# A Fourier transform and two expert layers in one kernel: GpSimd makes the block sums of x2, asb goes ahead of the difference on VectorE, and the two weighings of a pair stand two rounds apart

## The chip, the core and the metric

The kernel runs on one core of a Trainium2 chip. A core has five engines that run side by side, each through its own instructions in a fixed order: TensorE (PE in the profile, its weight loads PEld), VectorE (DVE), ScalarE (ACT), GpSimd (POOL) and SyncE (SP, which here starts transfers). They wait for each other by semaphores. The metric is the device time of one execution in microseconds (us). Three runs of the kernel before took 2791.44, 2799.14 and 2800.77 us, a median of 2799.14 us.

## The reference

Three things are computed one after the other, in float32:

```python
X = np.fft.fft(x, axis=1); X = np.fft.fft(X, axis=2)   # x is 8 x 3072 x 256
x1 = X.real.reshape(8 * 3072, 256)
h = x1 @ w_in                     # 256 -> 2048
x2 = (h - np.tanh(h)) @ w_out     # 2048 -> 256
h = x2 @ w_in2                    # 256 -> 1024
e = np.exp(h - h.max(-1)); sm = e / (e.sum(-1) + 1e-9)
solu = h * sm
ln = (solu - mean(solu)) / np.sqrt(var(solu) + 1e-6) * g_ln
out = ln @ w_out2                 # 1024 -> 256
```

## The kernel before, in words

**Precision.** A float32 value is split into a rounded half and a rest. ScalarE makes the rounded half (`rnd`, L166), and VectorE or GpSimd makes the rest by a subtraction (`rest`, L169). A product then takes three matmuls: high by high, high by low, low by high.

**Stages.** The first part of the program does the transform along the sequence. The main loop, which takes nearly the whole time, runs over 48 groups (`n`, `NG`) of 256 pairs of tokens and, in each, over the 16 blocks of 128 columns of the first hidden layer (`j`, `NM`). One pass of the loop body is called a step here, 16 steps of one `n` a big round; steps are numbered 0 to 15 in it. (The short title of the change says "round" for a step.)

**One step on the first layer.** TensorE first adds the odd part of the hidden block of the step before (`parity(.., 1)`, L879, 3 matmuls) and then starts the even part of this step's block (`even`, L879, 3 matmuls) in one of three PSUM buffers `h`. VectorE makes the first half of `h` of the step before (`act_in`, L904, written over the odd half), the sum `asb` of this step's even part and a correction (`lead`, L897), and, for the block of two steps before, the difference of `h` and its tanh (`act_out`, L921). The odd part of a block may be added only after `asb` has read its even part, so TensorE waits for `asb` at the start of the next step. ScalarE takes the tanh (L912) and rounds the difference into the high half of `gh` (L166); the low half of `gh` comes from GpSimd (L169), or, for the two blocks in eight that `LOWS` names, from VectorE (`low_by_vector`). Three steps after a block was started, its `gh` goes through six matmuls into `x2p` (`o1`, L941); the last two of the six need the low half.

**The second layer.** When the 16 blocks of a group are done, `x2p` holds x2 for 512 tokens, four tiles `t` of 128 tokens, handled as two pairs `p` of tiles 2p and 2p+1. The product of a pair with `w_in2` is done by Strassen's scheme with seven block products instead of eight: the four blocks A11, A12, A21, A22 of x2 (`xb`) and the four sums S1 to S4 (`sum_x2`, L957, one instruction for both pairs of a group) are split into high and low halves (`split_x2`: ScalarE the high, GpSimd the low, tile `xs`), three splits for each pair. TensorE multiplies them into two PSUM banks (`product`, L970), with `xs` as the loaded weights and the low half in the third pass. VectorE copies and combines the banks to `u` (`block`, L992). Then, for each tile: the exponential (`power`, ScalarE, L1007), the product of `u` and the exponential with its sum (`weigh`, VectorE, L1016, 128x1024, both inputs in SBUF), the square with its sum (`square`, ScalarE, L1027), three small steps for the scale (`scale`, GpSimd, L1035 to L1041), the transpose of 32x32 blocks (`turn`, VectorE, L1046, with a transfer out and back in four parts on SyncE's queue), the splits of the turned tile (`split_moved`, ScalarE and GpSimd, tile `ut`), the output product (`outp`, TensorE, L1074 and L1081), and the scaled store (`scaled`, `store`, L1091, L1095).

**What sets the order.** It is written out by hand. `layer2` is called at three places of each step ("ahead", "early", "late") with lists of (`back`, work): the work of pair `p` is issued in step 20 + `back` + 8p of the loop. So `back` 8, 9, 10 and 12 mean steps 4, 5, 6 and 0 of a big round for even p, and 12, 13, 14 and 8 for odd p. Each engine takes its instructions in the order in which the steps issue them; nothing reorders them later.

Of the kernel before, what the change touches and what calls it, by code (L numbers as in the profile page):

```python
# [32 lines left out]
NG = B * GPB  # L33
# [106 lines left out]
def fft2_moe_moe_kernel(  # L140
    ctx: ExitStack, tc: tile.TileContext, xr, x8, xn, xn8, w_in, w_out, w_in2, w_out2, g_ln, tt, t8, ft, out
):
    nc = tc.nc
# [725 lines left out]
    bank_b = p_pr.tile([P, HF], F32, tag="b", name="bank_b")  # L869

    hs, as_, ts_, gs = {}, {}, {}, {}
    LOWS = (0, 5)
    x2p, x2s = {}, {}

    def parity(n, m, u):
# [19 lines left out]
    def lead(n, m):  # L895
        asb = as_[n, m] = wk1.tile([P, GP], F32, tag="asb", name=f"asb{n}_{m}")
        nc.vector.scalar_tensor_tensor(  # L897
            out=asb, in0=zg[n][1], scalar=wnu[:, m : m + 1], in1=hs[n, m][:, 0], op0=ALU.mult, op1=ALU.add
        )
# [52 lines left out]
    def sum_x2(b):  # L952
        a0, a1, op = {
            S1: (A21, A22, ALU.add), S2: (S1, A11, ALU.subtract),
            S3: (A11, A21, ALU.subtract), S4: (A12, S2, ALU.subtract),
        }[b]
        nc.vector.tensor_tensor(out=xb[:, b], in0=xb[:, a0], in1=xb[:, a1], op=op)  # L957

    def split_x2(p, b0, b1):
        x = xb[:, b0 : b1 + 1, p % 2]  # L960
# [52 lines left out]
    def weigh(t, h=None):  # L1013
        e, st = es.pop(t), sts[t]
        u = us[t][0]
        nc.vector.scalar_tensor_tensor(  # L1016
            out=u, in0=u if h is None else h, scalar=-1.0 if h is None else 1.0, in1=e,
            op0=ALU.mult, op1=ALU.mult, accum_out=st[:, 2:3],
        )
        us[t] = (u, e)  # L1020

    def square(t):

        u, e = us[t]
        st = sts[t]
        nc.scalar.activation(out=st[:, 3:4], in_=st[:, 2:3], func=AF.Copy, scale=-1.0 / (32 * FF2))
        nc.scalar.activation(  # L1027
            out=e, in_=u, func=AF.Square, scale=1.0 / 32, bias=st[:, 3:4], accum_out=st[:, 6:7]
        )

    def scale(t):

        st = sts[t]
        g = nc.gpsimd
        g.tensor_scalar(  # L1035
            out=st[:, 4:5], in0=st[:, 1:2], scalar1=1e-9, scalar2=1e-3, op0=ALU.add, op1=ALU.mult
        )
        g.tensor_scalar(
            out=st[:, 5:6], in0=st[:, 4:5], scalar1=st[:, 4:5], scalar2=st[:, 6:7], op0=ALU.mult, op1=ALU.add
        )  # L1040
        g.tensor_tensor(out=st[:, 10:11], in0=st[:, 5:6], in1=mhalf, op=ALU.pow)  # L1041
# [66 lines left out]
    def layer2(step, place):  # L1108

        works = {  # L1110
            "ahead": (
                (20, lambda p: store(2 * p + 1)),
                (24, lambda p: store(2 * p)),
                (2, lambda p: product(p, bank_a, A12, B21)),
                (4, lambda p: product(p, bank_b, S3, T3)),
                (6, lambda p: product(p, bank_b, A22, T4)),
                (1, lambda p: nc.scalar.copy(out=bank_b, in_=bank_a)),
                (3, lambda p: (new_u(2 * p), kept(2 * p, 1))),
            ),
            "early": (  # L1120
                (17, lambda p: outp(2 * p + 1, 0)),
                (19, lambda p: outp(2 * p + 1, 1)),
                (21, lambda p: outp(2 * p, 0)),
                (23, lambda p: outp(2 * p, 1)),
                (3, lambda p: block(2 * p, 0, bank_a, False, True)),
                (5, lambda p: block(2 * p + 1, 1, bank_a, True, True)),
                (6, lambda p: block(2 * p + 1, 0, bank_b, False, False)),
                (7, lambda p: block(2 * p, 1, bank_a, True, False)),
                (7, lambda p: power(2 * p + 1)),
                (8, lambda p: (power(2 * p), weigh(2 * p + 1))),  # L1130
                (9, lambda p: weigh(2 * p)),
                (10, lambda p: (square(2 * p + 1), scale(2 * p + 1), turn(2 * p + 1))),
                (12, lambda p: (square(2 * p), scale(2 * p), turn(2 * p))),
                (14, lambda p: split_moved(2 * p + 1, 0)),
                (16, lambda p: split_moved(2 * p + 1, 1)),
                (18, lambda p: split_moved(2 * p, 0)),
                (20, lambda p: split_moved(2 * p, 1)),
                (-1, lambda p: split_x2(p, A11, A12)),
                (1, lambda p: split_x2(p, S2, S3)),
                (3, lambda p: split_x2(p, A22, S4)),  # L1140
            ),
            "late": (
                (0, lambda p: product(p, bank_a, A11, B11, True)),
                (2, lambda p: product(p, bank_b, S2, T2)),
                (4, lambda p: product(p, bank_a, S1, T1, True)),
                (6, lambda p: product(p, bank_a, S4, B22)),
                (4, lambda p: (new_u(2 * p + 1), kept(2 * p + 1, 1))),
                (19, lambda p: scaled(2 * p + 1)),
                (23, lambda p: scaled(2 * p)),
            ),  # L1150
        }
        for back, work in works[place]:
            p = pair_at(step, back)
            if p is not None:
                work(p)
# [11 lines left out]
    for step in range(steps + 3):  # L1167
        n, j = divmod(step, NM)
        if step in at_ab:
            special(at_ab[step])  # L1170
        if 0 < step <= steps:
            parity(*divmod(step - 1, NM), 1)
        if step < steps:
            even(n, j)
        if 0 < step <= steps:
            act_in(*divmod(step - 1, NM))
        if n == 0:
            lead(n, j)
        lag = 3 if step < NM else 2
        for s in range(out_done, min(step - lag + 1, steps)):  # L1180
            act_out(*divmod(s, NM))
        out_done = max(out_done, min(step - lag + 1, steps))
        if step - 1 in wo2_at:
            split_wo2(wo2_at.index(step - 1), True)
        layer2(step, "ahead")
        if 0 < n < NG:
            lead(n, j)
        if 0 < n < NG:
            for blk in {3: (S1,), 4: (S2, S3), 5: (S4,)}.get(j, ()):
                sum_x2(blk)  # L1190
        layer2(step, "early")
        if NM <= step < steps + 2:
            low_by_vector(*divmod(step - 2, NM))
        if step in at_o1:
            special(at_o1[step])
        if step in (NM, NM + 2):
            mean_wo2((step - NM) // 2)
        if step == NM + 2:
            nc.tensor.matmul(bank_b, wi2[:, B11, 0, :P], wi2[:, B11, 0], start=True, stop=True)
        s1 = step - 5 if step < NM else step - 3  # L1200
        for s in (range(o1_done, min(s1 + 1, steps))):
            o1(*divmod(s, NM))
        o1_done = max(o1_done, min(s1 + 1, steps))
        layer2(step, "late")
        if step in (3, 5, 7, 9):
            c, part = divmod((step - 3) // 2, 2)
            split_wo1(c + 2, wo1_raw[c + 2], slice(part * 2, part * 2 + 2))
        if step == NM:
            raw1.close()
            mv = pool(mv_stack, "mv", 2, side="right")  # L1210
        if step in wi2_sums:
            sum_wi2(nc.vector, wi2_sums[step])
        if step in wi2_splits:
            split_wi2(nc.gpsimd, wi2_splits[step])
        if step in (2, 3):
            load_wo2(step - 2)
        if step == 3:
            for k in range(2):
                load_wi2(k)
        if 8 <= step < NM:  # L1220
            gain_wo2(step - 8)
        if step in (NM + 3, NM + 4):
            center_wo2(step - NM - 3)
        if step in wo2_at:
            split_wo2(wo2_at.index(step), False)
        if step == NM + 12:
            nc.scalar.copy(out=pas, in_=pa)
        if step == NM + 20:
            special_out()
        if n == NG - 1 and j == 9:  # L1230

            b12 = zp.tile([P, HF], F32, tag="zf", name="b12")
            nc.sync.dma_start(out=b12, in_=wi2_d[0][:, HF:])
        if n == NG - 1 and j == 12:
            split_halves(nc.gpsimd, wt[0][:, 0, 0], wt[0][:, 1, 0], b12)
        if step == NM + 30:
            make_identity(nc, ident)
        if 1 <= n and n + 1 < NG:
            if j == 3:
                load_z(n + 1)  # L1240
            for u in range(2):
                if j == 7:
                    sum_z(n + 1, u, nc.gpsimd)
                if j == 11:
                    whole, hi, lo = by_half(n + 1, u)
                    rnd(hi, whole)
                    rest(nc.gpsimd, lo, whole, hi)
# [158 lines left out]
```

## Time and profile before

| what | value |
|---|---|
| median of three runs | 2799.14 us |
| time of the profiled execution | 2796.38 us |
| its span (first to last instruction) | 2794.6 us |
| granted TensorE clock, share of full speed | 0.996 |
| busy: PE / DVE / ACT / POOL | 96% / 84% / 73% / 70% |
| slices 5 to 39 of 40, busy tenths: PE / DVE / ACT / POOL | 9 / 8 / 7 / 7 |

The span is cut into 40 equal slices in the profile, and from the fifth on they hardly differ: the main loop repeats one pattern. "Busy" of TensorE counts each matmul from its start to its modelled end, and neighbours overlap, so the idle time that matters is found by comparing the starts of matmuls and not by the 96%. One big round is therefore read instruction by instruction below, between 1234 and 1271 us.

### The profile page before, as it was taken

How to read it: one execution, taken by the hardware profiler on the slowest of the kernel's cores; microseconds unless marked ns; L12 is line 12 of the kernel's file. 1: busy time of each engine (PE TensorE's matmuls, PEld its weight loads, DVE VectorE, ACT ScalarE, POOL GpSimd, SP SyncE). 2: the span in 40 equal slices, each digit the busy share in tenths (PEclk: the TensorE clock that was granted, in tenths of full speed). 3: DMA queues.
4: the chain of work that ended last, by engine and by line, in shares of the span. 5: the costliest groups of instructions: out<-in, count | busy, mean ns of one | idle time of the engine just before them, and what ended most of it. 6: DMA issues, size and time to landing. Idle time of an engine off the chain costs nothing.

```text
span 2794.6 us, 47353 instructions
## 1 busy us (share of the span) xinstructions
PE 2675.7 (96%) x15073; PEld 2343.8 (84%) x15073; DVE 2346.1 (84%) x4577; ACT 2030.1 (73%) x3990; POOL 1949.3 (70%) x2121
## 2 busy tenths in 40 slices
PE   9999999999999999999999999999999999999998
PEld 5677888888888888888888888888888888888887
DVE  8978888888888888888888888888888888888885
ACT  3467777777777777777777777777777777777775
POOL 0057777777777777777777777777777777777774
PEclk9999999999999999999999999999999999999999
DMA  9942443434434444443434434344344444434342
GB/s 363 365 156 50 95 99 89 106 88 102 94 89 104 92 99 92 98 99 89 105 87 99 99 89 105 86 105 99 84 103 92 99 92 98 99 84 108 88 99 50
DMA packets 882651, 302.97 MB, mean 108 GB/s; under 512 B 788544, under 2 KB 844144, under 8 KB 879104
## 3 DMA queue, kind: packets, MB, share of 16 engines
q1 hardware_dynamic: 879792, 293.45, 43.4%
q10 hardware_dynamic: 2304, 6.42, 0.6%
q8 instruction: 119, 1.95, 0.3%
q14 instruction: 132, 1.08, 0.1%
q0 software_dynamic: 304, 0.07, 0.0%
HBM read 161.26 MB, written 138.60 MB: 107 GB/s over the span
## 4 chain that ended last, share of the span: by engine, by line
PE 59%; DVE 13%; POOL 12%; ACT 11%; issue 4%; DMA 1%; POOLq 0%; ACTq 0%; SPq 0%; DVEq 0%
PE x2p L941 22%; PE h L879 11%; POOL gh L169 10%; PE po L1074 7%; PE bank_b L970 7%; PE bank_a L970 5%; DVE u L1016 4%; PE po L1081 3%; ACT t L912 3%; ACT e L1007 3%; DVE xb L957 3%; ACT gh L166 2%; POOL ut L169 2%; DVE h L904 2%; PE pz L486 1%
## 5 line engine op out<-in xcount | busy, mean ns | idle before, releaser
L169 POOL TENSOR_TENSOR gh<-t,gh 128x512 fp32r<-128x512 f32 x584 | 891.2, 1526 | 406.7 <-ACT gh L166 343.3
L941 PE MATMUL x2p<-gh,wo 128*128 128x512 f32 x4608 | 1150.4, 383 | 19.1 <-POOL gh L169 15.9
L941 PEld LDWEIGHTS x2p<-gh,wo 128*128 128x128 f32 x4608 | 829.4, 190 | 160.3 <-POOL gh L169 56.7
L912 ACT ACTIVATE t<-h 128x512 f32<-128x512 f32 x762 | 455.1, 597 | 634.0 <-DVE h L904 449.6
L879 PEld LDWEIGHTS h<-zs,wt 128*128 128x128 f32 x4572 | 626.5, 192 | 143.9 <-DVE asb L897 105.5
L879 PE MATMUL h<-zs,wt 128*128 128x256 f32 x4572 | 645.0, 277 | 81.1 <-DVE asb L897 80.3
L904 DVE SCALAR_TENSOR_TENSOR h<-asb,h 128x256 f32<-128x256 f32 x762 | 325.2, 427 | 399.6 <-PE h L879 396.7
L169 POOL TENSOR_TENSOR ut<-um,ut 128x512 fp32r<-128x512 f32 x372 | 479.2, 1288 | 175.5 <-PE x2p L941 133.5
L1074 PE MATMUL po<-wo,ut 128*128 128x512 f32 x1528 | 522.2, 383 | 1.9 <-DVE o L1095 1.1
L1081 PE MATMUL po<-wo,ut 128*128 128x256 f32 x1528 | 416.5, 273 | 0.0
L921 DVE TENSOR_TENSOR t<-h,t 128x512 f32<-128x512 f32 x578 | 394.0, 682 | 0.0
L166 ACT ACTIVATE gh<-t 128x512 fp32r<-128x512 f32 x584 | 367.3, 629 | 5.5 <-DVE t L921 4.3
L897 DVE SCALAR_TENSOR_TENSOR asb<-nb,wnu,h 128x256 f32<-128x256 f32 x762 | 358.7, 471 | 0.7 <-PE h L879 0.6
L1016 DVE SCALAR_TENSOR_TENSOR u<-u,e 128x1024 f32<-128x1024 f32 x188 | 340.7, 1812 | 0.0
L1074 PEld LDWEIGHTS po<-wo,ut 128*128 128x128 f32 x1528 | 289.9, 190 | 32.9 <-DVE o L1095 1.6
L970 PE MATMUL bank_a<-wi,xs 128*128 128x512 f32 x1128 | 310.6, 384 | 0.0
L1081 PEld LDWEIGHTS po<-wo,ut 128*128 128x128 f32 x1528 | 293.4, 192 | 0.2
L169 POOL TENSOR_TENSOR xs<-xb,xs 128x256 fp32r<-128x256 f32 (+1 forms) x282 | 233.7, 829 | 17.9 <-ACT xs L166 9.6
L970 PE MATMUL bank_b<-wi,xs 128*128 128x512 f32 x846 | 229.9, 380 | 0.2 <-POOL xs L169 0.2
L166 ACT ACTIVATE ut<-um 128x512 fp32r<-128x512 f32 x372 | 229.8, 618 | 0.0
L1046 DVE STREAM_TRANSPOSE tb<-u 128x1024 f32<-128x1024 f32 x186 | 229.8, 1235 | 0.0
L970 PEld LDWEIGHTS bank_a<-wi,xs 128*128 128x128 f32 x1128 | 206.7, 190 | 26.1 <-POOL xs L169 0.2
(156 smaller groups left out, 3099.4 us busy)
## 6 DMA issues: line engine op xcount, KB each, us to landing
mv_d<-tb SPq DMA_DIRECT2D x186, 512.0 KB, 3.1
um<-mv_d SPq DMA_DIRECT2D x744, 128.0 KB, 3.8
out<-o SPq DMA_DIRECT2D x192, 128.0 KB, 1.7
x<-xr SPq DMA_DIRECT2D x23, 1024.0 KB, 10.8
zf<-z_d SPq DMA_DIRECT2D x64, 128.0 KB, 3.7
z_d<-zt ACTq DMA_DIRECT2D x16, 392.0 KB, 6.0
wi<-w_in SPq DMA_DIRECT2D x6, 1024.0 KB, 7.4
z_d<-zt SPq DMA_DIRECT2D x16, 384.0 KB, 9.8
```

Of the source, the lines that this page charges most:

```text
L166: nc.scalar.activation(out=o, in_=i, func=AF.Copy)
L169: eng.tensor_tensor(out=o, in0=i, in1=hi.bitcast(F32), op=ALU.subtract)
L879: nc.tensor.matmul(in_pairs(hs[n, m][:, 0]), wt[c][:, hw, u, o : o + P], in_turn(zs[:, hz, u]), start=(u == 0 and i == 0), stop=(i == 2), ...
L897: nc.vector.scalar_tensor_tensor(out=asb, in0=zg[n][1], scalar=wnu[:, m : m + 1], in1=hs[n, m][:, 0], op0=ALU.mult, op1=ALU.add)
L904: nc.vector.scalar_tensor_tensor(out=h[:, 1], in0=as_.pop((n, m)), scalar=2.0, in1=h[:, 0], op0=ALU.mult, op1=ALU.subtract)
L912: nc.scalar.activation(out=t, in_=h, func=AF.Tanh)
L921: nc.vector.tensor_tensor(out=g, in0=h, in1=t, op=ALU.subtract)
L941: nc.tensor.matmul(in_pairs(x2p[n][mt]), wo1[c][:, hw, k, mt * P : (mt + 1) * P], in_turn(gh[:, hg]), start=(m == 0 and i == 0), stop=(m = ...
L970: nc.tensor.matmul(in_pairs(bank), xs[:, hx, xs_at[a]], in_turn(wi2[:, b, hw]), start=(start and q == 0), stop=(q == 2), skip_group_check= ...
L1016: nc.vector.scalar_tensor_tensor(out=u, in0=u if h is None else h, scalar=-1.0 if h is None else 1.0, in1=e, op0=ALU.mult, op1=ALU.mult, a ...
L1074: nc.tensor.matmul(in_pairs(po), ut[:, 0, ks], wo2[:, k].rearrange("p h x n -> p (x n) h"), start=(k == 0), stop=False,)
L1081: nc.tensor.matmul(in_pairs(po[:, :D]), ut[:, 1, ks], wo2[:, k, :, 0].rearrange("p h n -> p n h"), start=False, stop=(k == NK2 - 1),)
```

## The change

Four things are edited in the main loop. `lead`, which makes `asb`, is issued directly behind `act_in` in all big rounds, where it stood behind the differences and the "ahead" list in all but the first. The four sums of x2's blocks go from VectorE to GpSimd, and S2 is issued in step 3 with S1 (S3 in step 4, S4 in step 5, as before). The list of layer 2 puts `turn` of tile 2p+1 at 9 (it was 10) and `weigh` of tile 2p at 10 (it was 9). `LOWS` names blocks 1 and 5 in eight instead of 0 and 5.

```diff
-    LOWS = (0, 5)
+    LOWS = (1, 5)
...
-        nc.vector.tensor_tensor(out=xb[:, b], in0=xb[:, a0], in1=xb[:, a1], op=op)
+        nc.gpsimd.tensor_tensor(out=xb[:, b], in0=xb[:, a0], in1=xb[:, a1], op=op)
...
-                (9, lambda p: weigh(2 * p)),
-                (10, lambda p: (square(2 * p + 1), scale(2 * p + 1), turn(2 * p + 1))),
+                (9, lambda p: turn(2 * p + 1)),
+                (10, lambda p: (weigh(2 * p), square(2 * p + 1), scale(2 * p + 1))),
...
-        if n == 0:
+        if step < steps:
             lead(n, j)
...
         if 0 < n < NG:
-            lead(n, j)
-        if 0 < n < NG:
-            for blk in {3: (S1,), 4: (S2, S3), 5: (S4,)}.get(j, ()):
+            for blk in {3: (S1, S2), 4: (S3,), 5: (S4,)}.get(j, ()):
                 sum_x2(blk)
```

On VectorE, before, from the start of step 4 of big round 23 to its step 6 (`h23_3` is block 3 of group 23, `u87` and `u86` are the tiles 2p+1 and 2p, `tb87` the turned tile, `xb` x2 issues are the sums S2 and S3, then S4):

```order
L904 SCALAR_TENSOR_TENSOR h23_3_15422<-asb23_3_15433,h23_3_15422 128x256
L921 TENSOR_TENSOR t23_2_15427<-h23_2_15388,t23_2_15427 128x512
L1095 SCALAR_TENSOR_TENSOR o82_15457<-po82_15369,st82_14639,o82_15457 128x256
L897 SCALAR_TENSOR_TENSOR asb23_4_15481<-nb23_14824,wnu_123,h23_4_15468 128x256
L957 TENSOR_TENSOR xb_1233<-xb_1233 128x256 x2
L1016 SCALAR_TENSOR_TENSOR u87_15350,st87_15351<-u87_15350,e87_15445 128x1024
L904 SCALAR_TENSOR_TENSOR h23_4_15468<-asb23_4_15481,h23_4_15468 128x256
L921 TENSOR_TENSOR t23_3_15473<-h23_3_15422,t23_3_15473 128x512
L897 SCALAR_TENSOR_TENSOR asb23_5_15515<-nb23_14824,wnu_123,h23_5_15503 128x256
L957 TENSOR_TENSOR xb_1233<-xb_1233 128x256
L1016 SCALAR_TENSOR_TENSOR u86_15278,st86_15279<-u86_15278,e86_15485 128x1024
L904 SCALAR_TENSOR_TENSOR h23_5_15503<-asb23_5_15515,h23_5_15503 128x256
```

And the same stretch of VectorE now:

```order
L904 SCALAR_TENSOR_TENSOR h23_3_15422<-asb23_3_15429,h23_3_15422 128x256
L897 SCALAR_TENSOR_TENSOR asb23_4_15476<-nb23_14825,wnu_123,h23_4_15469 128x256
L921 TENSOR_TENSOR t23_2_15427<-h23_2_15388,t23_2_15427 128x512
L1095 SCALAR_TENSOR_TENSOR o82_15458<-po82_15369,st82_14641,o82_15458 128x256
L1016 SCALAR_TENSOR_TENSOR u87_15350,st87_15351<-u87_15350,e87_15445 128x1024
L904 SCALAR_TENSOR_TENSOR h23_4_15469<-asb23_4_15476,h23_4_15469 128x256
L897 SCALAR_TENSOR_TENSOR asb23_5_15510<-nb23_14825,wnu_123,h23_5_15503 128x256
L921 TENSOR_TENSOR t23_3_15474<-h23_3_15422,t23_3_15474 128x512
L1046 STREAM_TRANSPOSE tb87_15527<-u87_15350 128x1024
L904 SCALAR_TENSOR_TENSOR h23_5_15503<-asb23_5_15510,h23_5_15503 128x256
L897 SCALAR_TENSOR_TENSOR asb23_6_15553<-nb23_14825,wnu_123,h23_6_15546 128x256
L1016 SCALAR_TENSOR_TENSOR u86_15280,st86_15281<-u86_15280,e86_15485 128x1024
```

The three sums are gone, `asb` stands next after `h`, and between the two weighings (L1016) there are now two steps with the transpose in between.

On GpSimd, before, in steps 2 to 6 of the same big round (`gh23_k` is the low half of block k, `ut85_0` and `ut85_1` the halves of a turned tile, `xs` the low halves of x2's blocks, first A11 and A12, then S2 and S3):

```order
L169 TENSOR_TENSOR ut85_0_15404<-um85_15247,ut85_0_15404 128x512
L169 TENSOR_TENSOR gh23_1_15430<-t23_1_15393,gh23_1_15430 128x512
L169 TENSOR_TENSOR xs_1234<-xb_1233,xs_1234 128x256
L169 TENSOR_TENSOR gh23_2_15476<-t23_2_15427,gh23_2_15476 128x512
L169 TENSOR_TENSOR ut85_1_15488<-um85_15247,ut85_1_15488 128x512
L169 TENSOR_TENSOR gh23_3_15511<-t23_3_15473,gh23_3_15511 128x512
L169 TENSOR_TENSOR xs_1234<-xb_1233,xs_1234 128x256
L169 TENSOR_TENSOR gh23_4_15547<-t23_4_15508,gh23_4_15547 128x512
```

And now:

```order
L169 TENSOR_TENSOR gh23_0_15398<-t23_0_15361,gh23_0_15398 128x512
L169 TENSOR_TENSOR ut85_0_15405<-um85_15213,ut85_0_15405 128x512
L957 TENSOR_TENSOR xb_1233<-xb_1233 128x256 x2
L169 TENSOR_TENSOR xs_1234<-xb_1233,xs_1234 128x256
L169 TENSOR_TENSOR gh23_2_15479<-t23_2_15427,gh23_2_15479 128x512
L957 TENSOR_TENSOR xb_1233<-xb_1233 128x256
L169 TENSOR_TENSOR ut85_1_15488<-um85_15213,ut85_1_15488 128x512
L169 TENSOR_TENSOR gh23_3_15513<-t23_3_15474,gh23_3_15513 128x512
L957 TENSOR_TENSOR xb_1233<-xb_1233 128x256
L169 TENSOR_TENSOR xs_1234<-xb_1233,xs_1234 128x256
L169 TENSOR_TENSOR gh23_4_15556<-t23_4_15508,gh23_4_15556 128x512
```

The low half of block 1 has left GpSimd and that of block 0 has come; S1 and S2 (x2), S3 and S4 stand in front of `xs`, of `ut85_1` and of the second `xs`. The order on TensorE and SyncE is the same as before, row for row, and on ScalarE too but for which blocks' `gh` reads `h` instead of `t`.

## Rows read from the trace of the kernel before

**Rows 1.** The page, busy time and share of each engine.

```profile
PE 2675.7 (96%) x15073; PEld 2343.8 (84%) x15073; DVE 2346.1 (84%) x4577; ACT 2030.1 (73%) x3990; POOL 1949.3 (70%) x2121
```

**Rows 2.** Windows, instructions of L897 alone (asb, one per step): stretch, length, busy.

```profile
300.00:2700.00 2400.00, 334.09 (x710) 1.00 0.43 96
```

**Rows 3.** Timeline of PE, steps 4 to 6: start, us, what, [idle before <-releaser].

```profile
1234.69 1.46 PE L941 MATMUL x2p<-gh,wo 128*128 128x512 f32 x6
1235.98 0.81 PE L970 MATMUL bank_a<-wi,xs 128*128 128x512 f32 x3
1236.63 0.83 PE L879 MATMUL h<-zs,wt 128*128 128x256 f32 x6
1237.30 0.38 PE L1074 MATMUL po<-wo,ut 128*128 128x512 f32 x1
...
1238.61 1.46 PE L941 MATMUL x2p<-gh,wo 128*128 128x512 f32 x6
1241.73 0.94 PE L879 MATMUL h<-zs,wt 128*128 128x256 f32 x6 [1.66 <-DVE asb L897]
...
1243.24 1.80 PE L941 MATMUL x2p<-gh,wo 128*128 128x512 f32 x6
1244.87 0.81 PE L970 MATMUL bank_b<-wi,xs 128*128 128x512 f32 x3
```

**Rows 4.** Timeline of DVE, the same steps 4 and 5.

```profile
1234.55 0.43 DVE L904 SCALAR_TENSOR_TENSOR h<-asb,h 128x256 f32<-128x256 f32 x1 [0.86 <-PE h L879]
1234.89 0.68 DVE L921 TENSOR_TENSOR t<-h,t 128x512 f32<-128x512 f32 x1
...
1235.88 0.47 DVE L897 SCALAR_TENSOR_TENSOR asb<-nb,wnu,h 128x256 f32<-128x256 f32 x1
1236.27 1.85 DVE L957 TENSOR_TENSOR xb<-xb 128x256 f32<-128x256 f32 x2
1238.04 2.30 DVE L1016 SCALAR_TENSOR_TENSOR u<-u,e 128x1024 f32<-128x1024 f32 x1
...
1241.59 0.41 DVE L957 TENSOR_TENSOR xb<-xb 128x256 f32<-128x256 f32 x1
1241.93 1.22 DVE L1016 SCALAR_TENSOR_TENSOR u<-u,e 128x1024 f32<-128x1024 f32 x1
```

**Rows 5.** Timeline of POOL, the same steps.

```profile
1236.37 1.47 POOL L169 TENSOR_TENSOR gh<-t,gh 128x512 fp32r<-128x512 f32 x1 [1.09 <-PE x2p L941]
1237.97 1.28 POOL L169 TENSOR_TENSOR ut<-um,ut 128x512 fp32r<-128x512 f32 x1
1242.02 2.26 POOL L169 TENSOR_TENSOR gh<-t,gh 128x512 fp32r<-128x512 f32 x1 [2.77 <-ACT gh L166]
1244.24 0.73 POOL L169 TENSOR_TENSOR xs<-xb,xs 128x256 fp32r<-128x256 f32 x1
```

**Rows 6.** Timeline of all engines, steps 13 and 14, the second half of the round.

```profile
1266.83 1.28 POOL L169 TENSOR_TENSOR ut<-um,ut 128x512 fp32r<-128x512 f32 x1
1266.98 2.22 DVE L1016 SCALAR_TENSOR_TENSOR u<-u,e 128x1024 f32<-128x1024 f32 x1
1268.07 2.25 POOL L169 TENSOR_TENSOR gh<-t,gh 128x512 fp32r<-128x512 f32 x1
1270.38 0.70 PE L941 MATMUL x2p<-gh,wo 128*128 128x512 f32 x2 [0.28 <-POOL gh L169]
```

**Rows 7.** Groups by shape: POOL's operations, count, busy us, mean ns, idle before.

```profile
L169 POOL TENSOR_TENSOR gh<-t,gh 128x512 fp32r<-128x512 f32 x584 | 891.2, 1526 | 406.7 <-ACT gh L166 343.3 <-PE x2p L941 49.9 <-issue 4.0
L169 POOL TENSOR_TENSOR xs<-xb,xs 128x256 fp32r<-128x256 f32 x188 | 138.5, 737 | 14.2 <-ACT xs L166 6.1 <-PE h L879 5.6
L169 POOL TENSOR_TENSOR xs<-xb,xs 128x384 fp32r<-128x384 f32 x94 | 95.2, 1013 | 3.7 <-ACT xs L166 3.6
L272 POOL TENSOR_TENSOR zc<-zf 128x128 f32<-128x128 f32 x184 | 70.1, 418 | 0.0
```

**Rows 8.** Timeline of ACT, step 4: the high half of gh.

```profile
1235.61 0.63 ACT L166 ACTIVATE gh<-t 128x512 fp32r<-128x512 f32 x1
```

## The prediction

> **What bounds the kernel now.** I read the page first, then TensorE's own timeline, then what stood on the other engines where TensorE stopped.
>
> On the page TensorE is busy 96% of the span, far ahead of VectorE with 84%, ScalarE with 73% and GpSimd with 70% [rows 1]. That figure hides its stops, since matmuls overlap. So I compare starts. Six matmuls of `x2p` take 1.29 us (1234.69 to 1235.98), three of a bank 0.65, six of `h` 0.67, and half an output product with the `po` matmuls 1.31 (1237.30 to 1238.61) [rows 3]. Eight steps hold eight times `x2p` and `h`, seven bank products and four output halves: 8 x 1.96 + 7 x 0.65 + 4 x 1.31 = 25.47 us. A big round of 16 steps would take 50.94 us if TensorE never stopped. Its real length comes from counting `asb`, one per step: 710 in 2400 us [rows 2], so 54.08 us. TensorE loses 3.14 us in each big round.
>
> Where? Call T the start of step 4, 0.67 us before the first of [rows 3], 1234.02. The six `x2p` that start at 1238.61 should be followed at 1239.90; the next `h` starts at 1241.73, waiting for `asb`: 1.83 us lost. The six `x2p` at 1243.24 take 1.63 instead of 1.29: 0.34 lost to the low half of `gh` [rows 3]. In the second half of the round the last two `x2p` matmuls start at 1270.38 behind GpSimd's `gh` [rows 6], some 0.45 us late. These three make 2.6 of the 3.14 us; the rest is spread over pauses of a tenth.
>
> The cause of the first stands on VectorE. At T + 0.53 come `h`, the difference, a store's sum and `asb`, 1.72 us for the four (1234.55 to 1236.27), then two block sums that take 1.85 us together, though one alone takes 0.41, and a weighing of 2.30 us that takes 1.22 elsewhere [rows 4]. Sum two stands still while GpSimd has its `gh` (1.47 us), the weighing while GpSimd has `ut` (to 1239.25), and the `gh` dispatched at 1242.02 behind a running weighing takes 2.26 instead of 1.28 [rows 5]. So a VectorE instruction with two SBUF inputs and a GpSimd instruction don't run side by side: one waits until the other is done. [Rows 6] also show who goes first: the weighing dispatched at 1266.98 waits for `ut`, and when that ends it runs before the `gh` that GpSimd dispatched at 1268.07. The Trainium skill says the same of the pair of ports that the two share ("SBUF — State Buffer", Who interferes with whom): an exclusive lock, the loser stands still for the whole instruction. By a shared bandwidth both would have stretched; the trace shows one whole instruction added to the other (2.25 is 1.28 and most of a weighing), and on this I build below.
>
> **The change part by part.** *VectorE loses the sums.* Three of the four stand in steps 4 and 5, 1.85 and 0.41 us before the two weighings [rows 4], and only they and the weighing make `asb` of step 5 late. *`asb` moves up* by two instructions, from T + 1.86 to T + 0.87, where the even part is just done; in step 5 it comes behind `h` alone. *The second weighing* leaves step 5 for step 6, and a transpose takes its place; it has one input, so I take it not to hold GpSimd.
>
> The new order on VectorE, with the same durations: `h` at T + 0.53, `asb`, difference (from 1.26 to 1.94), store, first weighing from T + 2.25 to 3.4. Then `h` at 3.4, `asb` of step 5 done at about 4.2. TensorE wants it at the start of step 6, which is T + 2.61 + 3.27 = T + 5.88. So the 1.83 us are gone with more than 1 us to spare. In the second half of the round the `gh` of step 13 no longer meets a weighing: 1.28 instead of 2.25 [rows 6], which is more than the 0.45 us it was late. The second weighing now meets the `gh` of step 14. By the sums below that one ends about 4.6 us after the start of its step, and TensorE wants it at 3.27 + 0.67 + 1.31 + 0.86 = 6.1. I count nothing lost in the second half.
>
> *GpSimd gets the sums*, and here I expect the new wait. No row shows this sum on GpSimd. The nearest is its subtraction of the same 128x256 size, 737 ns; the bounds are 418 ns for half the size and 1013 ns for one and a half [rows 7]. I take 0.74. S1 and S2 in step 3 are free: the low half of block 1 has left that step for VectorE, where it stands in a step without weighing, and GpSimd idled before step 4 for 1.09 us [rows 5]. S3 and S4 are not free. GpSimd's queue from step 4 on, after T:
>
> - the high half of `gh` (0.63 us, [rows 8]) is done at 1.94 + 0.67 = 2.6; the first weighing has the ports since 2.25. A `gh` behind a weighing ends 1.07 + 1.28 us after the weighing's start ([rows 4, 5]: 1241.93, 1244.28): 4.60.
> - S3 0.74, `ut` 1.28, the next `gh` 1.28, each starting some 0.04 before the last one's recorded end: 7.8. TensorE needs this `gh` for the fifth `x2p` matmul of step 6, at 5.88 + 0.67 + 0.65 + 0.86 = 8.06, less 0.17 for the hand-over (`gh` ended 1244.28, its matmul ran about 1244.45). Just in time.
> - S4 is next, and behind it `xs`, the low halves of S2 and S3. But the second weighing is dispatched at about T + 7.74 (5.88 + 0.53, then `h`, `asb`, difference), while that `gh` runs, and as in [rows 6] goes first: to 8.84. S4 to 9.57, `xs` (0.73) to 10.26, its matmul at 10.43.
>
> TensorE wants these low halves in the third pass of the product S2 x T2, at 5.88 + 0.67 + 0.65 + 1.29 + 0.43 = 8.92. Before, `xs` stood directly behind `gh` (1244.24 to 1244.98) and that product began at 1244.87 [rows 3, 5]: no wait. Now it waits 10.43 - 8.92 = 1.5 us. Behind it GpSimd has `gh`, the scale's steps, `ut`, `xs` and `zc`, and it has caught up by step 10, since TensorE slid by the same 1.5.
>
> The sum: of 3.14 us lost per big round 1.5 remain, so 1.64 are saved. With 45 such rounds (the first two and the last are partly without this work) that is 74 us. From the profiled execution's own 2796.4 us (1.8 outside its span; 0.1% under the median of the three runs, 2799.1) comes 2722 us. With sums of 0.42 us the wait is 0.86 and the time 2694; with 1.01 it is 2.06 and 2748.
>
> The Trainium skill speaks against moving such a sum ("GPSIMD Engine Reference", 4.1 Engine selection): two-input elementwise work belongs on VectorE, GpSimd being about twice as slow. The rows agree in kind, 0.74 to 0.41. By its ratio in 3.1 of that page, 1.96, I estimate a sum at 0.80 us and the time at 2728.
>
> **Rivals.** *No new wait (0.25).* GpSimd has 1.09 and 2.77 us of idle time before its two `gh` [rows 5], and what I put down to one instruction of order could fall out otherwise: if S4 and `xs` get the ports before the second weighing, `xs` ends at 9.2 and TensorE waits 0.45, which gives 2675; without any wait it is 45 x 3.14 = 141 us, 2655. Against it: in [rows 6] the waiting weighing goes first.
>
> *Slow sums eat the gain (0.09).* If a sum on GpSimd takes as long as its mean `gh`, 1.53 us [rows 7], S3 and S4 bring 1.58 more, TensorE waits 3.08 and the time is 2793. Between the bounds' 2748 and this lies most of what I give it, say 2775. It decides from 1.55 us a sum. Against it: 512 elements take 1.28 undisturbed, so 256 can't well take more.
>
> *The wait moves to `gh` and grows (0.06).* With `asb` first, the difference ends 0.39 us later in every step, and so do both halves of `gh`. In the four steps behind weighings GpSimd delivers at the limit (0.34 and 0.45 late now, [rows 3, 6]); if the later weighing of step 6 and 14 doesn't free it there, each of the four loses 0.39, 1.56 in all, on top of 1.5 for `xs` and the old 0.45. That is 3.5 us in place of 3.14, and 2796 + 45 x 0.37 = 2813 us. It decides once the four add up to over 1.2. Against it: a transpose and not a weighing stands there now.
>
> **How the numbers follow.** The forecast as worked out has 0.60, its own range 2694 to 2748. The range of 0.8 takes in the case without a wait and a part of the slow sums: 2655 to 2770. About 0.3% (8 us) can be told from no change. Faster: 0.60 + 0.25 + 0.06 of the second rival, 0.91. Within 0.3%: 0.03. Slower: 0.06.
>
> **What would show it.** Right: `h` on TensorE never waits for `asb`; a big round of 52.4 us; one new wait per round, of a `bank_b` matmul in step 6 for GpSimd's `xs`, about 1.5 us; weighings of 1.2 us in step 4; sums on GpSimd of 0.74, S4 near 1.8 because it is held; the `gh` of step 13 at 1.28. Wrong: rounds of 51 us without that wait (first rival), sums over 1 us (second), or `x2p` waiting for `gh` in several steps (third). If `asb` still holds TensorE, my reading of VectorE's queue is wrong.

## The result, and the profile after

The changed kernel took 2727.7 us in the median of four runs (2725.32 to 2731.39), against 2795.38 us of the kernel before: a ratio of 0.976, 95% interval 0.973 to 0.978. The forecast was 2722 us. The profiled execution has a span of 2729.3 us.

The page, busy time by engine, against [rows 1]: VectorE has lost 146 us, GpSimd has gained 135.

```profile
PE 2650.9 (97%) x15073; PEld 2345.3 (86%) x15073; DVE 2200.1 (81%) x4389; ACT 2035.8 (75%) x3990; POOL 2084.7 (76%) x2309
```

How long is a big round now? Below is the window view of L897 alone (stretch, length, busy, count), from 300 to 2500 us, so that the main loop fills it in every kernel.

```profile
300.00:2500.00 2200.00, 319.66 (x670) 1.00 0.43 99
```

There are 670 steps in 2200 us, so a round of 16 takes 52.54 us. The kernel before has 651 in the same stretch, 54.07 us. The difference of 1.53 us, 45 times, is 69 us.

TensorE's timeline in steps 4 to 6 of one big round, which answers to [rows 3]; step 4 starts at T = 1210.18.

```profile
1210.18 0.83 PE L879 MATMUL h<-zs,wt 128*128 128x256 f32 x6
...
1214.77 1.46 PE L941 MATMUL x2p<-gh,wo 128*128 128x512 f32 x6
1216.07 0.83 PE L879 MATMUL h<-zs,wt 128*128 128x256 f32 x6
1216.73 0.81 PE L970 MATMUL bank_a<-wi,xs 128*128 128x512 f32 x3
1217.38 1.46 PE L941 MATMUL x2p<-gh,wo 128*128 128x512 f32 x6
1218.68 0.59 PE L970 MATMUL bank_b<-wi,xs 128*128 128x512 f32 x2
1220.38 0.48 PE L970 MATMUL bank_b<-wi,xs 128*128 128x512 f32 x1 [1.11 <-POOL xs L169]
```

The `h` of step 6 follows `x2p` after 1.30 us, as the matmuls alone take; before, it came 1.83 us later than that. The six `x2p` at 1217.38 run through in 1.30. The only stop is in front of the third pass of `bank_b`: two passes take 0.43 us, so it was due at 1219.11 and started at 1220.38, 1.27 us late.

VectorE in the same steps, against [rows 4]:

```profile
1211.05 0.48 DVE L897 SCALAR_TENSOR_TENSOR asb<-nb,wnu,h 128x256 f32<-128x256 f32 x1
...
1212.44 1.22 DVE L1016 SCALAR_TENSOR_TENSOR u<-u,e 128x1024 f32<-128x1024 f32 x1
...
1213.91 0.47 DVE L897 SCALAR_TENSOR_TENSOR asb<-nb,wnu,h 128x256 f32<-128x256 f32 x1
...
1214.90 1.24 DVE L1046 STREAM_TRANSPOSE tb<-u 128x1024 f32<-128x1024 f32 x1
...
1217.93 1.81 DVE L1016 SCALAR_TENSOR_TENSOR u<-u,e 128x1024 f32<-128x1024 f32 x1
```

And GpSimd, against [rows 5]:

```profile
1208.82 1.55 POOL L957 TENSOR_TENSOR xb<-xb 128x256 f32<-128x256 f32 x2
1211.00 0.73 POOL L169 TENSOR_TENSOR xs<-xb,xs 128x256 fp32r<-128x256 f32 x1 [0.63 <-PE h L879]
1212.93 1.87 POOL L169 TENSOR_TENSOR gh<-t,gh 128x512 fp32r<-128x512 f32 x1 [1.20 <-ACT gh L166]
1214.76 0.73 POOL L957 TENSOR_TENSOR xb<-xb 128x256 f32<-128x256 f32 x1
1215.45 1.28 POOL L169 TENSOR_TENSOR ut<-um,ut 128x512 fp32r<-128x512 f32 x1
1216.69 1.28 POOL L169 TENSOR_TENSOR gh<-t,gh 128x512 fp32r<-128x512 f32 x1
1217.93 0.73 POOL L957 TENSOR_TENSOR xb<-xb 128x256 f32<-128x256 f32 x1
1218.62 1.70 POOL L169 TENSOR_TENSOR xs<-xb,xs 128x256 fp32r<-128x256 f32 x1
```

`asb` of step 5 is done at 1214.4, 1.7 us before TensorE can want it. From 1212.93 to 1220.32 GpSimd has no pause: `gh` held by the first weighing, S3, `ut`, `gh`, S4, and then the split of S2 and S3, 1.70 us long because the second weighing holds it. Set beside each other, the two lists show it: S4 and the second weighing are dispatched in the same hundredth, S4 runs its undisturbed 0.73, the weighing takes 1.81 instead of 1.22, and when it ends, the split gets its turn.

In all, by the groups (count, busy, mean ns, idle before), the sum takes 741 ns on GpSimd, and a split of this size 979 instead of 737 [rows 7]:

```profile
L957 POOL TENSOR_TENSOR xb<-xb 128x256 f32<-128x256 f32 x188 | 139.2, 741 | 3.7
L169 POOL TENSOR_TENSOR xs<-xb,xs 128x256 fp32r<-128x256 f32 x188 | 184.0, 979 | 127.9 <-ACT xs L166 98.9 <-PE h L879 28.8
L169 POOL TENSOR_TENSOR gh<-t,gh 128x512 fp32r<-128x512 f32 x584 | 812.7, 1392 | 257.2 <-ACT gh L166 243.9 <-issue 3.4 <-POOL gh L169 2.3
```

In the second half of the round the `gh` of step 13, 2.25 us long in [rows 6], is undisturbed (GpSimd's timeline again):

```profile
1243.60 1.28 POOL L169 TENSOR_TENSOR gh<-t,gh 128x512 fp32r<-128x512 f32 x1
```

### The profile page after: what moved, and what is told of

Read it like the earlier page. It is cut to its first block, busy times and chain, and to the rows that moved or that the text cites. A ratio compares the mean times of both kernels' runs of the same rounds, so it can differ in the third digit from the quotient of the medians.

```text
span 2729.3 us, 47917 instructions
## 1 busy us (share of the span) xinstructions
PE 2650.9 (97%) x15073; PEld 2345.3 (86%) x15073; DVE 2200.1 (81%) x4389; ACT 2035.8 (75%) x3990; POOL 2084.7 (76%) x2309
## 4 chain that ended last, share of the span: by engine, by line
PE 74%; POOL 14%; DVE 5%; issue 4%; DMA 2%; ACT 1%; SPq 0%; POOLq 0%; DVEq 0%; ACTq 0%
PE x2p L941 29%; PE h L879 16%; PE po L1074 10%; PE bank_a L970 7%; PE bank_b L970 6%; PE po L1081 5%; POOL gh L169 5%; POOL xs L169 4%; POOL xb L957 3%; POOL ut L169 2%; DVE cv L452 1%; DVE pm L457 1%; DVE sm L447 1%; DMA tts<-tt 0%; DMA x<-xr 0%
## 5 line engine op out<-in xcount | busy, mean ns | idle before, releaser
L941 PE MATMUL x2p<-gh,wo 128*128 128x512 f32 x4608 | 1125.9, 380 | 1.4 <-POOL gh L169 1.4
L169 POOL TENSOR_TENSOR gh<-t,gh 128x512 fp32r<-128x512 f32 x584 | 812.7, 1392 | 257.2 <-ACT gh L166 243.9
L879 PEld LDWEIGHTS h<-zs,wt 128*128 128x128 f32 x4572 | 633.3, 191 | 49.0 <-DVE asb L897 2.9
L169 POOL TENSOR_TENSOR ut<-um,ut 128x512 fp32r<-128x512 f32 x372 | 477.8, 1284 | 5.1 <-ACT ut L166 5.1
L169 POOL TENSOR_TENSOR xs<-xb,xs 128x256 fp32r<-128x256 f32 (+1 forms) x282 | 279.1, 990 | 133.9 <-ACT xs L166 101.2
L897 DVE SCALAR_TENSOR_TENSOR asb<-nb,wnu,h 128x256 f32<-128x256 f32 x762 | 363.5, 477 | 1.9 <-PE h L879 1.9
L970 PE MATMUL bank_b<-wi,xs 128*128 128x512 f32 x846 | 242.1, 386 | 53.4 <-POOL xs L169 52.7
L1016 DVE SCALAR_TENSOR_TENSOR u<-u,e 128x1024 f32<-128x1024 f32 x188 | 279.9, 1489 | 0.0
```

The costliest lines, as they stand in the source:

```text
L169: eng.tensor_tensor(out=o, in0=i, in1=hi.bitcast(F32), op=ALU.subtract)
L879: nc.tensor.matmul(in_pairs(hs[n, m][:, 0]), wt[c][:, hw, u, o : o + P], in_turn(zs[:, hz, u]), start=(u == 0 and i == 0), stop=(i == 2), ...
L897: nc.vector.scalar_tensor_tensor(out=asb, in0=zg[n][1], scalar=wnu[:, m : m + 1], in1=hs[n, m][:, 0], op0=ALU.mult, op1=ALU.add)
L941: nc.tensor.matmul(in_pairs(x2p[n][mt]), wo1[c][:, hw, k, mt * P : (mt + 1) * P], in_turn(gh[:, hg]), start=(m == 0 and i == 0), stop=(m = ...
L970: nc.tensor.matmul(in_pairs(bank), xs[:, hx, xs_at[a]], in_turn(wi2[:, b, hw]), start=(start and q == 0), stop=(q == 2), skip_group_check= ...
L1016: nc.vector.scalar_tensor_tensor(out=u, in0=u if h is None else h, scalar=-1.0 if h is None else 1.0, in1=e, op0=ALU.mult, op1=ALU.mult, a ...
```

## The experiments

The theory (Q in the expectations below) is that TensorE's stops are set by who stands in front of whom in two short queues, VectorE's and GpSimd's, and by the two engines holding each other; not by how much either has to do. All kernels were timed beside the kernel before on the same chip. Ratios are to that kernel; a big round's length is counted from `asb` between 300 and 2500 us as above.

### What is left of the wait

**All sums in step 3.**

```diff
-            for blk in {3: (S1, S2), 4: (S3,), 5: (S4,)}.get(j, ()):
+            for blk in {3: (S1, S2, S3, S4)}.get(j, ()):
```

> The changed kernel with all four sums of x2 issued on GpSimd in step 3. Theory Q (queue order: the 1.4 us that a big round still loses is the low half of S2 and S3, held on GpSimd behind S4 and the second weighing): the sums end about when step 4 starts, that split comes directly behind the gh of step 6 and nearly always before the weighing; the wait goes, rounds of 51.0 us, 2728 - 45 x 1.4 = 2665 us (2655 to 2685). Theory L (GpSimd's load: it has the same work and makes TensorE wait somewhere): 2720 to 2735 us, with the wait at another instruction.

2664.83 us, ratio 0.954 (0.952 to 0.956), round 51.16 us. GpSimd's timeline, steps 3 to 6:

```profile
1181.06 2.94 POOL L957 TENSOR_TENSOR xb<-xb 128x256 f32<-128x256 f32 x4
1183.95 0.74 POOL L169 TENSOR_TENSOR xs<-xb,xs 128x256 fp32r<-128x256 f32 x1
1185.17 1.87 POOL L169 TENSOR_TENSOR gh<-t,gh 128x512 fp32r<-128x512 f32 x1 [0.48 <-ACT gh L166]
1186.99 1.29 POOL L169 TENSOR_TENSOR ut<-um,ut 128x512 fp32r<-128x512 f32 x1
1188.23 1.29 POOL L169 TENSOR_TENSOR gh<-t,gh 128x512 fp32r<-128x512 f32 x1
1189.46 0.75 POOL L169 TENSOR_TENSOR xs<-xb,xs 128x256 fp32r<-128x256 f32 x1
```

The four sums fill what was a pause around the start of step 4, the split of S2 and S3 follows `gh` at once and is not held. GpSimd has the same instructions as in the changed kernel; only two of them stand elsewhere. The round is 1.38 us shorter, which is the whole of what was still lost to that wait, and theory L, which puts it down to GpSimd's load, falls for it. The kernel is 2.3% under the changed one.

**S4 one step later.**

```diff
-            for blk in {3: (S1, S2), 4: (S3,), 5: (S4,)}.get(j, ()):
+            for blk in {3: (S1, S2), 4: (S3,), 6: (S4,)}.get(j, ()):
```

> The changed kernel with S4 issued one step later, in step 6, so that on GpSimd the split of S2 and S3 follows gh directly. Theory Q: the split is dispatched with the second weighing, as S4 was, and GpSimd goes first as it did there; no wait, 2665 us (2660 to 2700; 2700 where the weighing goes first). Theory L (GpSimd's load): 2720 to 2735 us.

2689.38 us, ratio 0.962 (0.960 to 0.964), round 51.69. The wait for the split is gone, and 61% of what the kernel above gained is there. But a smaller one has come, TensorE's waits in total, times, longest:

```profile
PE x2p L941 <- POOL gh L169: 13.4, 44, 0.6
```

By the starts of its matmuls TensorE loses 0.5 us in each step 10: without the pause of step 6, GpSimd's row of work behind it (S4 is now part of it) has not caught up by then. So its load does count from step 6 on, and half of theory L stands: there the queue has no slack to take one sum more.

**The second weighing without a second SBUF input.**

```diff
     def weigh(t, h=None):
         e, st = es.pop(t), sts[t]
         u = us[t][0]
+        if h is None and t % 2 == 0:
+            nc.vector.transpose(out=e, in_=u)
+            nc.vector.memset(st[:, 2:3], 0.0)
+            us[t] = (u, e)
+            return
```

> The changed kernel, but the weighing of each tile 2p is replaced by an instruction with one SBUF input and nearly its length (a 32x32 block transpose of u into e, 1.24 us, and a memset of the sum); so the weighted product of these tiles is left out. Theory Q with ports that two-input VectorE instructions and GpSimd hold in turn: nothing holds the split of S2 and S3 in step 6 any more, it ends 0.74 after S4, and of the 1.4 us that TensorE waits 0.45 stay: 2728 - 43 = 2685 us (2675 to 2700). Theory N (no holding; GpSimd is late by its queue alone): 2722 to 2733 us, the split still at 1.7.

2681.68 us, ratio 0.959 (0.958 to 0.961), round 51.61. VectorE's instruction in the place of the weighing and GpSimd's two beside it:

```profile
1198.34 1.23 DVE L1017 STREAM_TRANSPOSE e<-u 128x1024 f32<-128x1024 f32 x1
```

```profile
1198.34 0.75 POOL L957 TENSOR_TENSOR xb<-xb 128x256 f32<-128x256 f32 x1
1199.04 0.74 POOL L169 TENSOR_TENSOR xs<-xb,xs 128x256 fp32r<-128x256 f32 x1
```

Both engines run side by side at full pace, with the same length of instruction on VectorE (the kernel leaves out the weighted product of these tiles). The instruction put in is of another kind than the weighing, but the kind is not what counts: `asb`, the same operation as the weighing with one of its inputs in PSUM, runs beside a split of GpSimd in the changed kernel above (1211.05, 0.48 and 1211.00, 0.73), and neither is longer for it. So it is the second SBUF input that makes them hold each other, and of the 1.4 us some 0.9 are the weighing's (the round is 0.93 shorter) and the rest is S4's place in the queue. Theory N falls.

### One part undone

**The sums back on VectorE.**

```diff
-        nc.gpsimd.tensor_tensor(out=xb[:, b], in0=xb[:, a0], in1=xb[:, a1], op=op)
+        nc.vector.tensor_tensor(out=xb[:, b], in0=xb[:, a0], in1=xb[:, a1], op=op)
```

> The changed kernel with the four sums back on VectorE, in the steps of the changed kernel (S1 and S2 in step 3, S3 in 4, S4 in 5). Theory Q: with asb ahead of them and the weighings apart, VectorE has the time: S3 alone delays asb of step 5 by 0.4 us, inside its spare 1.7; the split of S2 and S3 stands directly behind gh again, so TensorE waits for neither: rounds near 51.2, 2665 to 2690 us. Theory V (the sums had to leave VectorE for asb to be in time): TensorE waits 1 us or more for asb in step 5, and the time is 2740 to 2790 us.

2720.29 us, ratio 0.973 (0.972 to 0.975), round 52.46: neither what Q gave nor V. As Q had it, TensorE waits neither for `asb` nor for the split. It waits for something that I had left out. VectorE and TensorE, end of step 3:

```profile
1200.76 0.88 DVE L957 TENSOR_TENSOR xb<-xb 128x256 f32<-128x256 f32 x2
1201.55 0.74 DVE L992 CUSTOM_DVE_ANT_0 u<-bank_a,u,st 128x512 f32<-128x512 f32 x1
...
1202.22 0.69 DVE L169 TENSOR_TENSOR gh<-h,gh 128x512 fp32r<-128x512 f32 x1
```

```profile
1202.16 0.50 PE L879 MATMUL h<-zs,wt 128*128 128x256 f32 x3
1202.96 0.60 PE L879 MATMUL h<-zs,wt 128*128 128x256 f32 x3 [0.30 <-DVE gh L169]
```

S1 and S2 stand before the low half of block 1, which VectorE makes from `h`, and TensorE needs that one of three buffers for the even part of step 4. The last three matmuls, at 1202.96, should have come 0.33 after the first three, at 1202.49. The same happens at the start of step 8 behind block 5.

**The sums on VectorE and LOWS (0, 5).** The edit above, and:

```diff
-    LOWS = (1, 5)
+    LOWS = (0, 5)
```

> The changed kernel with the sums on VectorE and LOWS as before (blocks 0 and 5). With the sums on VectorE and LOWS (1, 5) TensorE waited for neither asb nor a split but, at the start of steps 4 and 8, for a PSUM buffer of h that VectorE still reads for the low half of blocks 1 and 5 (0.6 and 0.73 us a round). Theory H (two jobs in one step: S1, S2 and the low half of block 1 stand together in step 3): the 0.6 go, the 0.73 stay, 2720 - 27 = 2693 us (2680 to 2705). Theory V (VectorE is too full with the sums): 2712 to 2725 us, the wait at another step.

2701.73 us, ratio 0.967 (0.966 to 0.969), round 51.92. With block 1 on GpSimd the wait in step 4 is gone, that in step 8 stays, as expected; of the two waits of TensorE for VectorE's `gh` one is left (38.8 us at its matmuls with LOWS (1, 5), and now):

```profile
PE h L879 <- DVE gh L169: 22.2, 45, 0.6
```

This kernel is 1% faster than the changed one, with the sums on VectorE (S2 a step earlier than in the kernel before). So they did not have to leave VectorE, once `asb` stands ahead of them and the weighings are apart: these two of the four edits bring 93 us with S2 in step 3, more than all four do (68).

**LOWS alone undone**, with the sums on GpSimd.

```diff
-    LOWS = (1, 5)
+    LOWS = (0, 5)
```

> The changed kernel with LOWS as before, blocks 0 and 5. Theory Q: step 3 on GpSimd then has a gh in front of S1 and S2, which end at about T + 2.2, and the split of A11 and A12 (T + 2.9) comes 0.7 us late for the product of step 4; what follows slides with it: 0.7 to 1 us more lost, 2762 us (2745 to 2775). Theory R (LOWS is worth nothing): 2722 to 2733 us.

2759.04 us, ratio 0.987 (0.986 to 0.989), round 53.17. A `gh` stands in front of S1 and S2, and TensorE waits for both splits:

```profile
PE bank_b L970 <- POOL xs L169: 44.3, 47, 1.0
PE bank_a L970 <- POOL xs L169: 23.6, 47, 2.1
```

The small edit of LOWS is worth 31 us here, and costs 19 us where the sums are on VectorE: it clears step 3 on the engine that gets the sums and fills it on the other.

**The weighings one step apart again.**

```diff
-                (9, lambda p: turn(2 * p + 1)),
-                (10, lambda p: (weigh(2 * p), square(2 * p + 1), scale(2 * p + 1))),
+                (9, lambda p: weigh(2 * p)),
+                (10, lambda p: (square(2 * p + 1), scale(2 * p + 1), turn(2 * p + 1))),
```

> The changed kernel with the second weighing back one step behind the first, and the transpose with square and scale (9 and 10 as in the kernel before). Theory Q: the second weighing holds ut and gh of step 5 and 13; TensorE waits about 1.0 us for gh and 0.5 for the split in the first half, 0.45 for gh in the second: 2.0 us a big round instead of 1.4, 2728 + 27 = 2755 us (2740 to 2770). Theory W (the spacing only moves the collision to another step): 2722 to 2733 us.

2767.19 us, ratio 0.989 (0.988 to 0.991), round 53.41. As expected in kind, and at the upper end in size: by the starts of the matmuls the second half of the round loses 0.84 us where 0.45 was expected. With `asb` ahead the late `gh` of step 14 is later still, as the kernel with `asb` alone shows below. GpSimd's `ut` is now the one that is held, 1523 ns in the mean instead of 1284 in the changed kernel, and `gh` behind it is late in steps 6 and 14:

```profile
PE x2p L941 <- POOL gh L169: 55.6, 94, 1.0
PE bank_b L970 <- POOL xs L169: 12.0, 46, 0.9
```

**asb behind again.**

```diff
-        if step < steps:
+        if n == 0:
             lead(n, j)
...
         if 0 < n < NG:
+            lead(n, j)
             for blk in {3: (S1, S2), 4: (S3,), 5: (S4,)}.get(j, ()):
```

> The changed kernel with asb issued behind the difference and the ahead list again, as in the kernel before. Theory Q: without the sums asb of step 5 is done by T + 4.6 and wanted at 5.9, so its place is worth nothing: 2722 to 2732 us. Theory P (the place of asb is what freed TensorE): it waits for asb again, 1 us or more a round, 2770 us and above.

2720.10 us, ratio 0.973 (0.971 to 0.974), round 52.38: as good as the changed kernel or a little better, the two intervals overlapping by 0.001. TensorE's largest wait is the same one, and in the main loop none is for `asb`:

```profile
PE bank_b L970 <- POOL xs L169: 52.8, 47, 1.3
```

**All sums in step 3, asb behind.**

```diff
-        if step < steps:
+        if n == 0:
             lead(n, j)
...
         if 0 < n < NG:
-            for blk in {3: (S1, S2), 4: (S3,), 5: (S4,)}.get(j, ()):
+            lead(n, j)
+            for blk in {3: (S1, S2, S3, S4)}.get(j, ()):
```

> The kernel with all sums on GpSimd in step 3, and asb behind the difference and the ahead list as in the kernel before. Theory Q: once TensorE waits for nothing, the place of asb changes nothing: 2664 us (2656 to 2672). Theory P (asb ahead is needed there): TensorE waits for asb in the steps after a weighing, 2680 us and more.

2659.42 us, ratio 0.952 (0.950 to 0.954), round 51.01: the lowest time of all, within the interval of the kernel with `asb` ahead. Once the sums are off VectorE the place of `asb` is worth nothing; in both pairs of kernels the one with `asb` behind is a few us lower, too little to call it a gain.

### One part alone, on the kernel before

**The sums on GpSimd.**

```diff
-        nc.vector.tensor_tensor(out=xb[:, b], in0=xb[:, a0], in1=xb[:, a1], op=op)
+        nc.gpsimd.tensor_tensor(out=xb[:, b], in0=xb[:, a0], in1=xb[:, a1], op=op)
...
-            for blk in {3: (S1,), 4: (S2, S3), 5: (S4,)}.get(j, ()):
+            for blk in {3: (S1, S2), 4: (S3,), 5: (S4,)}.get(j, ()):
```

> The kernel before with one edit: the sums on GpSimd, in the steps of the changed kernel. Theory Q: asb is no longer late (1.8 us of 3.1), but the split of A11 and A12 comes 0.7 late behind the gh of block 1, and the two weighings one step apart hold GpSimd for 1.4 in the first half and 0.6 in the second: 2.6 us lost, 2780 us (2765 to 2797). Theory S (the sums on GpSimd are the change; the rest is finish): 2722 to 2745 us.

2755.61 us, ratio 0.986 (0.984 to 0.987), round 53.17. Better than I expected by 24 us, and worse than theory S. The waits are those expected, but by the starts of the matmuls that for A11 and A12 is half as long, 0.35 us: with `asb` behind, the difference and all that hangs on it come 0.39 us earlier, and I had taken the prices of kernels with `asb` ahead. In big round 24 that split starts 1.82 us into step 4, and 2.23 in the kernel with LOWS undone.

```profile
PE x2p L941 <- POOL gh L169: 36.1, 94, 1.2
PE bank_b L970 <- POOL xs L169: 12.6, 46, 1.3
```

**The spacing of the weighings.**

```diff
-                (9, lambda p: weigh(2 * p)),
-                (10, lambda p: (square(2 * p + 1), scale(2 * p + 1), turn(2 * p + 1))),
+                (9, lambda p: turn(2 * p + 1)),
+                (10, lambda p: (weigh(2 * p), square(2 * p + 1), scale(2 * p + 1))),
```

> The kernel before with one edit: the second weighing in 10 and the transpose in 9. Theory Q: the first weighing and the sums still hold asb of step 5 (1.8 us stay), but the gh of steps 5 and 13 meet no weighing: 0.34 and 0.57 us come back, 2796 - 41 = 2755 us (2742 to 2768). Theory W (the collision only moves): 2785 to 2800 us.

2754.94 us, ratio 0.986 (0.985 to 0.988), round 53.25. The wait for `asb` is what it was, 80.5 us at TensorE's matmuls, and that for `gh` has gone from 15.9 to 1.5 us.

**asb directly behind h.**

```diff
-        if n == 0:
+        if step < steps:
             lead(n, j)
...
-        if 0 < n < NG:
-            lead(n, j)
```

> The kernel before with one edit: asb directly behind h. Theory Q: asb of step 5 stands behind one instruction less on VectorE after the weighing, so it is 0.6 us earlier and 0.6 of the 1.83 us lost there come back: 2796 - 27 = 2769 us (2757 to 2780). Theory Z (its place is worth nothing, as in the changed kernel): 2788 to 2800 us.

2772.53 us, ratio 0.993 (0.991 to 0.995), round 53.41. The gain is 0.66 us a round in the profiled execution, the lowest of the four, and 0.48 by the medians. That is near the 0.6 expected, but by luck: the wait for `asb` has not lost 0.6 of its 1.83 us, it is nearly gone. TensorE's wait for it before,

```profile
PE h L879 <- DVE asb L897: 80.3, 49, 2.0
```

and TensorE's three largest now (that for `gh` was 15.9):

```profile
PE x2p L941 <- POOL gh L169: 29.2, 51, 1.1
PE bank_a L970 <- ACT bank_b L1117: 22.3, 46, 0.5
PE h L879 <- DVE asb L897: 6.1, 11, 1.7
```

What I had not seen is that S2 and S3 on VectorE are no longer held:

```profile
1223.86 0.75 DVE L957 TENSOR_TENSOR xb<-xb 128x256 f32<-128x256 f32 x2
```

They come as early in the step as before, but the difference, and with it GpSimd's `gh`, comes 0.4 us later. That `gh` starts 0.50 behind the sums (at 1224.36), where it started 0.10 behind them [rows 4, 5], so both sums run ahead of it, in 0.75 and not in 1.85 us. With `asb` 0.6 earlier this makes 1.7. By the starts of the matmuls, over big rounds 8 to 43, the loss in front of this `h` falls from 1.86 us to 0.21. Most of that is lost again elsewhere: step 6 now stops within `h` and in front of `bank_a`, which waits for ScalarE's copy of a bank (1.17 us, before 0.25), and step 14 for `gh` (0.85, before 0.56).

LOWS alone on the kernel before was not tried.

## Why the prediction was right, point by point

- **VectorE's late asb.** Predicted: the 1.83 us go, with over 1 us to spare. Measured: gone, 1.7 to spare. The prediction let the sums and the place of `asb` share this. The runs part them, and either alone does nearly all of it: of the 80.3 us that TensorE waits for `asb` in the kernel before, 5.0 are left with the sums alone on GpSimd and 6.1 with `asb` alone ahead. With the sums gone the place is worth nothing; with the sums there it gives 0.5 to 0.7 us a round, since other waits come in for most of what it frees.
- **The second half of the round.** Predicted: nothing lost. Measured: the `gh` of step 13 takes 1.28, and the 0.56 us lost in step 14 (mean of big rounds 8 to 43, by the starts) are gone.
- **The price of a sum on GpSimd.** Taken as 0.74 from a split of its size; measured 0.741. Against the 0.41 of an undisturbed sum on VectorE [rows 4] that is a ratio of 1.8. By the 1.96 of the Trainium skill ("GPSIMD Engine Reference", 3.1 Elementwise) the estimate would have been 0.80; the measurement decides.
- **The new wait.** Predicted: the third pass wanted at T + 8.92, ready at T + 10.43, 1.5 us lost. Measured at T + 8.93 and T + 10.20, 1.27 lost. The place and the kind of the wait came out; one step of its working did not: I let the second weighing go before S4, as in [rows 6], so that S4 would take 1.8. S4 went first with 0.73, the weighing took 1.81, and the split behind S4 was held, 1.70. In [rows 6] the weighing had waited for over a microsecond when the next GpSimd instruction was dispatched; here both came in the same hundredth. S4 first is half of the first rival's condition; the other half, the split ahead of the weighing too, was not met. That the end differs little is in part luck: either way the same three instructions run one after the other.
- **One engine holding the other.** Where a VectorE instruction with two SBUF inputs meets one of GpSimd, the later waits until the other is done; where VectorE's has one, nothing is added, as the experiment with one input shows (0.74 for the split beside it, 1.70 beside the weighing). With this the rule of the Trainium skill ("SBUF — State Buffer", Who interferes with whom) agrees.
- **The sum.** 1.64 us saved in each of 45 rounds was forecast, 74 us; measured 1.53 and 69 by the counts, 67.7 by the medians. It came so near because two misses nearly cancel. The new wait was taken 0.23 too long. The small pauses outside the three named places were let go with the rest, without a reason, and 0.33 us of them stay: 52.54 less 50.94 is 1.60 us lost, 1.27 of them in front of `bank_b`.
- **The rivals.** The one without a new wait is not what happened, but it is what the kernel with all sums in step 3 makes true: 2655 forecast for it, 2665 measured. The one of slow sums falls with the 0.741. The mechanism of the third, `gh` later by what `asb` moved, is real (with `asb` alone step 14 loses 0.85 us and not 0.56), but it has room in the changed kernel.

## What to carry to other kernels

When two engines hold each other, ask of each instruction that is moved not only how long it is but what it will meet, and what stands behind it in the queue that it joins: the four sums cost the same 3 us on GpSimd in every order tried, and the order alone was worth 63 us. As the changed kernel places them their move did not pay: with `asb` ahead and the weighings apart, the kernel with the sums on VectorE and the old LOWS took 2702 us, the changed one 2728, and the one with all sums on GpSimd in step 3 2665. Put moved work where the receiving engine pauses, in front of the point where its queue closes up, and count every engine's instructions from that point to the first consumer. An edit that frees an engine can be worth nothing beside another that frees the same wait: undo each part, since the parts do not add (here 40, 39 and 22 us alone).

## What had not been expected of the hardware

- A weighing and a GpSimd instruction dispatched in the same hundredth of a microsecond: GpSimd mostly went first, here with S4 and in the kernel with S4 in step 6 with the split. Of the meetings between 300 and 2500 us with starts at most 20 ns apart, 33 of 34 went so at S4 here and 58 of 61 at the splits there; what decides the others stays open. A weighing that had been waiting while the instruction before ran went first instead [rows 6].
- A split can lose more to being held once than it takes itself: 1.70 us in place of 0.73.
